# Two gated state-space convolutions on one core: fewer identity matmuls without a reader, in 26 places in place of 36

## The chip, the cores and the metric

The kernel runs on one core of a Trainium2 chip. The metric is the device time of one execution in microseconds (us); a kernel's time is the median of its runs. A core has TensorE (matmul and the load of its stationary operand), VectorE, ScalarE, GpSimd and SyncE, which here issues every DMA. The profile calls them PE and PEld, DVE, ACT, POOL and SP.

## The reference, cut to what matters

The input `x` has 2048 positions and 512 channels. Two state-space models (S4 with a pair of input and output vectors, S4D without) each make one kernel `K` of 2048 taps per channel from 128 complex modes, convolve it with the channel, and add a skip term. A gate mixes both.

```python
x = A_u
g = _sigmoid((x * gate_w).sum(-1, keepdims=True))
a = _A_ref(x, A_A_re, A_A_im, A_B_re, A_B_im, A_C_re, A_C_im, A_log_dt, A_Dskip)
b = _B_ref(x, B_log_A_real, B_A_imag, B_C_real, B_C_imag, B_log_dt, B_D_skip)
return g * a + (1 - g) * b

# inside _A_ref, and alike in _B_ref:
P = jnp.exp(logdA[:, :, None] * l[None, None, :])
K = jnp.einsum("dn,dnl,dn->dl", Cc, P, dB).real
...
Yf = Uf * Kf[None, :, :, :]
y = irfft2(Yf)[:, :, 0, :L]
y = transpose(y) + u * Dskip[None, None, :]
```

## The kernel before, in words

All arrays are float32. The 2 x 512 channels of kernels are handled in four groups of 128 channels (`q`, for the parameters) and eight half groups (`v`, 64 channels of each model). Work is staged:

- `params_t` and `params_c` make, for each `q`, angles and sizes of the modes (lines 375 to 490), from one load of raw parameters, `AB<-in_prm`.
- `anchors` makes exponentials for each `v` on ScalarE (lines 510 to 514).
- `chunk` runs eight times for each `v`. GpSimd multiplies angles and sizes out (L574, L583, L594, L602, and L560 for every fourth), ScalarE takes sines and cosines into PSUM tiles named `sd` (L614, L615, L616), VectorE multiplies both (L622, L627 into `QD`; L637, L632 into `E`), and TensorE sums over the modes with 32 small matmuls (L653, in the trace 64 records). Every second chunk ends with the skip term (L663) and a copy to SBUF (L675).
- `put` is the first half of a transform of length 2048 by matrices (L696, 32 matmuls of 64 x 64, 64 records), and `forward` the second half (L719). `stage1_u` and `stage2_u` do the same for the input `u`, whose spectrum goes to a DRAM scratch `ud` (L754, L756, L761).
- `stage2` multiplies the spectra (VectorE, L791 and L794) and begins the inverse transform (L803, L804), with the result copied (L807) to a DRAM scratch `wt` (L810).
- `gate` makes the gate's values (L865, L874, L876) and weighs the matrices of the last step with them. `final` loads `wt` back (L825), mixes both models in 32 matmul records (L836), and stores the output (L848).

The order is not written by hand. A planner, `Plan.run` (line 154), plays the operations against costs, latencies and due times and writes each engine's list of instructions. The numbers it works with were set by constants at the top of the file.

The change touches the table `FILL` (line 78). The planner counts the operations that it gives to TensorE. Where the count is a key of `FILL`, `Plan.spare` (line 140) puts matmuls ahead of that operation: the identity times a repeated identity, written to whichever PSUM tile (`ps` or `sd`) comes free first by the plan. Nothing reads the result. The value is a number of units, each 128 columns, up to four units in one matmul:

```python
for i in range(0, units, 4):
    k = min(4, units - i)
    self.keep(t[:, 0 : P * k].rearrange("p (k c) -> p k c", k=k), k)
```

All these matmuls stand on line 300 (L300 in the profile). `spare` takes no time in the plan, so its entries move no other operation; but its matmuls wait for their tile to come free like any other, and whoever writes the tile next waits for them. A float32 matmul is two weight loads and two matmuls in the trace. The PSUM tiles are six: `ps0` to `ps3` for results, `sd0` and `sd1` for sines and cosines.

Of the kernel before, what the change touches and what calls it, by code (L numbers as in the profile page):

```python
# [74 lines left out]
FW = -2.217  # L75


FILL = {1: 2, 3: 7, 5: 14, 17: 3, 49: 8, 50: 2, 51: 5, 54: 2, 55: 1, 88: 2, 160: 29, 161: 14, 162: 5, 199: 10, 201: 12, 213: 1, 275: 6, 304: 29, 22: 3, 32: 2, 33: 1, 52: 1, 53: 1, 57: 1, 58: 3, 66: 1, 68: 1, 71: 1, 181: 1, 189: 3, 196: 1, 198: 9, 200: 2, 202: 3, 244: 1, 249: 1}


def _flat(t):
# [27 lines left out]
class Plan:  # L109
# [44 lines left out]
    def run(self):  # L154
# [14 lines left out]
        while n < len(self.ops):  # L169
            nxt = 1e30  # L170
            for e in at:
# [32 lines left out]
                if e == "T":  # L204
                    if turn in FILL:
                        order.append(self.spare(FILL[turn], min((f, t, i) for t in ("ps", "sd") for f, i in free[t])))
                    turn += 1
# [842 lines left out]
```

## Time and profile before

| what | us |
|---|---|
| median of three runs | 500.5 |
| the three runs | 498.42, 500.87, 500.5 |
| the profiled execution | 499.39 |
| span of the profiled execution, first to last instruction | 497.6 |

The profile's page gives the busy time of each engine, the chain of waits that ended last, and the costliest groups of instructions. A row of the chain or of the timeline begins with the time from the span's start, then a length, both in us, then the engine, the line and what is written. Behind a row of the timeline stands in brackets how long the engine had been idle before it and what ended that. "issue" there is idle time for which the profile names no cause. `<-` reads "is made from". The transfers' page counts queue q1, which carries data, and queue q8, which carries instructions.

### The profile page before, as it was taken

The numbers are of one execution on the slowest core, as the hardware profiler recorded it, in microseconds if no ns is written. First come the engines' busy times: TensorE is split into PE (matmuls) and PEld (weight loads), VectorE is DVE, ScalarE is ACT, GpSimd is POOL, SyncE is SP. The second block draws the span as 40 slices with busy tenths as digits, with TensorE's granted clock in tenths as the row PEclk, the third lists the DMA queues.
The fourth block names the chain that finished last, engine by engine and source line by source line (L and its number), as shares of the span: only waits on it lengthen the run. The fifth ranks groups of instructions, "written<-read, shape, count | busy, mean of one in ns | idle before, by whom it ended". The sixth has DMA issues, their size and how long they took to land.

```text
span 497.6 us, 22093 instructions
## 1 busy us (share of the span) xinstructions
PE 449.3 (90%) x9718; PEld 386.4 (78%) x9718; DVE 396.6 (80%) x564; ACT 389.2 (78%) x598; POOL 394.3 (79%) x365
## 2 busy tenths in 40 slices
PE   4798897789999999999989998897999899999996
PEld 3497795678777788888568987487998799889975
DVE  5778797999939888999869988887979999884420
ACT  4679888989999887789999888786999977762111
POOL 4586986989979979999899999688979999950000
PEclk9999999999999999999999999999999999999999
DMA  8969755354554454443308676257245145863846
GB/s 278 397 195 282 218 162 157 102 167 119 157 172 141 132 178 142 127 118 119 107 4 253 184 237 237 50 199 222 67 149 177 62 130 169 268 205 108 302 141 234
DMA packets 69439, 85.46 MB, mean 172 GB/s; under 512 B 4704, under 2 KB 50144, under 8 KB 69088
## 3 DMA queue, kind: packets, MB, share of 16 engines
q1 hardware_dynamic: 69344, 84.06, 53.7%
q8 instruction: 76, 1.25, 1.1%
q14 instruction: 19, 0.16, 0.1%
HBM read 50.49 MB, written 33.59 MB: 169 GB/s over the span
## 4 chain that ended last, share of the span: by engine, by line
PE 41%; ACT 18%; DMA 16%; issue 8%; POOL 8%; DVE 8%; SPq 1%; DVEq 0%; ACTq 0%; POOLq 0%
PE ps L719 8%; PE ps L653 7%; PE ps L803 7%; PE ps L804 6%; PE ps L836 5%; PE ps L696 4%; DMA wt<-st 4%; DMA AB<-in_prm 3%; DMA c_g<-in_c_g 3%; ACT sd L614 3%; DMA X<-wt 3%; POOL E L602 2%; ACT x L615 2%; ACT sd L616 2%; DVE E L632 2%
## 5 line engine op out<-in xcount | busy, mean ns | idle before, releaser
L602 POOL TENSOR_TENSOR E<-AB 128x1024 f32<-128x1024 f32 x64 | 125.3, 1959 | 0.1
L803 PE MATMUL ps<-z,c_t 128*128 128x128 f32 x512 | 102.5, 282 | 3.7 <-DVE z L794 1.8
L804 PE MATMUL ps<-z,c_t 128*128 128x128 f32 x512 | 99.9, 277 | 0.9 <-DVE z L794 0.7
L622 DVE TENSOR_TENSOR QD<-sd,E 128x1024 f32<-128x1024 f32 x64 | 77.9, 1218 | 22.2 <-issue 7.6
L719 PE MATMUL ps<-F,c_g 128*128 128x128 f32 x640 | 83.9, 278 | 1.9 <-ACT F L708 1.2
L803 PEld LDWEIGHTS ps<-z,c_t 128*128 128x128 f32 x512 | 77.6, 191 | 8.9 <-DVE z L794 3.4
L719 PEld LDWEIGHTS ps<-F,c_g 128*128 128x128 f32 x640 | 76.2, 189 | 6.5 <-ACT F L708 1.8
L804 PEld LDWEIGHTS ps<-z,c_t 128*128 128x128 f32 x512 | 77.7, 192 | 2.6 <-DVE z L794 2.5
L632 DVE TENSOR_TENSOR E<-sd,E 128x1024 f32<-128x1024 f32 x64 | 77.8, 1215 | 0.8 <-ACT sd L616 0.8
L583 POOL TENSOR_TENSOR x<-pi,c_tm 128x512 int32<-128x512 int32 x64 | 68.0, 1064 | 11.0 <-ACT sd L616 10.1
L594 POOL TENSOR_TENSOR E<-AB 128x512 f32<-128x512 f32 x64 | 68.5, 1072 | 6.2 <-issue 2.5
L614 ACT ACTIVATE sd<-x 128x1024 f32<-128x1024 int32 x64 | 65.9, 1029 | 8.9 <-DVE QD L627 6.0
L653 PE MATMUL ps<-E 128*32 128x64 f32 x2048 | 64.7, 222 | 7.6 <-DVE E L632 3.3
L616 ACT ACTIVATE sd<-x 128x1024 f32<-128x1024 f32 x64 | 66.0, 1031 | 4.9 <-PE sd L300 2.2
L615 ACT ACTIVATE x<-x 128x1024 f32<-128x1024 int32 x64 | 67.8, 1060 | 1.3
L574 POOL TENSOR_TENSOR x<-gh 128x512 int32<-128x512 int32 x64 | 68.5, 1070 | 0.2
L807 ACT COPY st<-ps 128x512 f32<-128x512 f32 x64 | 37.6, 587 | 38.5 <-PE ps L804 24.9
L653 PE MATMUL ps<-QD 128*32 128x64 f32 x2048 | 63.5, 219 | 3.2 <-issue 3.2
L653 PEld LDWEIGHTS ps<-E 128*32 128x32 f32 x2048 | 48.2, 109 | 21.0 <-issue 10.5
L791 DVE TENSOR_TENSOR z<-ps,U 128x512 f32<-128x512 f32 x64 | 43.8, 685 | 25.0 <-PE ps L719 21.4
L653 PEld LDWEIGHTS ps<-QD 128*32 128x32 f32 x2048 | 49.9, 110 | 4.6 <-issue 4.6
L794 DVE SCALAR_TENSOR_TENSOR z<-ps,sgn,U 128x512 f32<-128x512 f32 x64 | 47.4, 742 | 0.0
(122 smaller groups left out, 786.1 us busy)
## 6 DMA issues: line engine op xcount, KB each, us to landing
U<-ud SPq DMA_DIRECT2D x32, 512.0 KB, 4.0
wt<-st SPq DMA_DIRECT2D x64, 256.0 KB, 2.9
X<-wt SPq DMA_DIRECT2D x26, 512.0 KB, 5.3
ud<-z SPq DMA_DIRECT2D x32, 256.0 KB, 3.6
U<-in_u SPq DMA_DIRECT2D x16, 256.0 KB, 4.6
ud<-z SPq DMA_DIRECT2D x32, 128.0 KB, 3.5
U<-in_uT SPq DMA_DIRECT2D x16, 256.0 KB, 3.5
out<-st SPq DMA_DIRECT2D x16, 256.0 KB, 5.4
```

The costliest lines, as they stand in the source:

```text
L574: G.tensor_tensor(xi()[:, :, 1, :].rearrange("n c (a b) -> n c a b", a=4), t[:, :, 0:4].unsqueeze(3).to_broadcast([P, NCK, 4, 8]), t[:, :, ...
L594: G.tensor_tensor(Ev()[:, :, 0, :].rearrange("n c (a b) -> n c a b", a=4), A1()[:, ca, ::-1].unsqueeze(3).to_broadcast([P, NCK, 4, 8]), BB ...
L602: G.tensor_tensor(Ev()[:, :, 1:3, :].rearrange("n c w t -> n c (w t)"), AA()[:, ca].rearrange("n c w a -> n (c w) a").unsqueeze(3).to_broa ...
L614: op("A", 0.96, e, lambda: A.activation(bv(sn), wv(xi()), AF.Sin, scale=SCL), r=[x], w=[sn], func="S")
L615: op("A", 0.96, e, lambda: A.activation(x.t, x.v(dt=I32), AF.Abs), w=[x])
L616: op("A", 0.96, e, lambda: A.activation(bv(cs), wv(qv(x)), AF.Sin, bias=HALF_PI, scale=-SCL), r=[x], w=[cs], func="S")
L622: lambda: V.tensor_tensor(ev(QD)[:, :, 0::2, :], bv(sn).rearrange("n w c t -> n c w t"), Ev()[:, :, 0::2, :], ALU.mult),
L632: lambda: V.tensor_tensor(Ev()[:, :, 0:2, :], bv(cs)[:, 0].unsqueeze(2).to_broadcast([P, NCK, 2, NJ]), Ev()[:, :, 0:2, :], ALU.mult),
L653: T.matmul(K4[32 * b : 32 * b + 32, gg, :], ev(QD if w else E)[:, c, 2, :], ev(QD if w else E)[:, c, 0:2].rearrange("n h t -> n (h t)"), s ...
L719: T.matmul(b.v("p (k m h e) -> p m k h e", k=2, m=4, h=32, e=2)[:, mm], Gw[:, m, :], Fv(F)[:, :, m, :].rearrange("p (k h) e -> p k h e", k=2),
L803: T.matmul(o, Tw[:, m, 0:128], zv(Z1), start=True, stop=False)
L804: T.matmul(o, Tw[:, m, 64:192], zv(Z2), start=False, stop=True)
```

## The change

The table has 26 entries in place of 36, and 159 units in place of 188.

```diff
-FILL = {1: 2, 3: 7, 5: 14, 17: 3, 49: 8, 50: 2, 51: 5, 54: 2, 55: 1, 88: 2, 160: 29, 161: 14, 162: 5, 199: 10, 201: 12, 213: 1, 275: 6, 304: 29, 22: 3, 32: 2, 33: 1, 52: 1, 53: 1, 57: 1, 58: 3, 66: 1, 68: 1, 71: 1, 181: 1, 189: 3, 196: 1, 198: 9, 200: 2, 202: 3, 244: 1, 249: 1}
+FILL = {1: 2, 3: 7, 5: 14, 17: 3, 49: 8, 50: 2, 51: 5, 54: 2, 160: 29, 161: 14, 162: 5, 199: 5, 201: 12, 213: 1, 275: 6, 304: 29, 22: 1, 52: 1, 58: 1, 68: 1, 189: 1, 196: 1, 198: 4, 202: 3, 244: 1, 249: 1}
```

Ten entries go (55, 88, 32, 33, 53, 57, 66, 71, 181, 200) and five shrink (199 from 10 units to 5, 198 from 9 to 4, and 22, 58 and 189 from 3 to 1). As matmuls of the program, thirteen go. In the trace of before the entries stand at these starts, in us: 22 at 44.77, 32 at 57.04, 33 at 58.95, 53 at 90.43, 55 at 95.14, 57 at 98.13, 58 at 100.20, 66 at 111.32, 71 at 118.99, 88 at 139.82, 181 at 280.73, 189 at 293.41, 198 at 308.40, 199 at 312.45 and 200 at 316.86.

No instruction of another engine moves, and TensorE's other operations keep their order. What its rows were and are is shown at three places. The number behind a tile's name is its buffer; DVE_49, Activation_49 and Pool_49 are the semaphores that VectorE, ScalarE and GpSimd raise.

TensorE at entry 32, between the input's transform (L696) and the taps (L653); `-` is before, `+` the change:

```order
 L696 MATMUL ps_101<-w_117,U_84 64x64 x2
 L696 MATMUL ps_100<-w_117,U_84 64x64 x2
-L300 MATMUL sd_105<-c_id 128x256 [waits DVE_49]
-L653 MATMUL ps_102<-E_72 32x64 [waits Pool_49]
+L653 MATMUL ps_102<-E_72 32x64 [waits DVE_49,Pool_49]
 L653 MATMUL ps_102<-E_72 32x64 x3
 L653 MATMUL ps_102<-QD_76 32x64 x4
```

The fill is gone and its wait for VectorE has moved to the first taps matmul, which waits for two engines now.

TensorE at entry 181, between the second half of a kernel's transform (L719) and the first half of the next (L696):

```order
 L719 MATMUL ps_101<-F_67,c_g 128x2x64 [waits Activation_49]
 L719 MATMUL ps_101<-F_67,c_g 128x2x64 x3
-L300 MATMUL ps_100<-c_id 128x128 [waits Activation_49]
 L696 MATMUL ps_100<-w_117,K_77 64x64 [waits Activation_49]
 L696 MATMUL ps_100<-w_117,K_77 64x64
```

Here the next operation had a wait of its own for the same engine, and keeps it.

TensorE at entry 199, between two runs of taps:

```order
 L300 MATMUL sd_105<-c_id 128x512 [waits DVE_49,Activation_49]
-L300 MATMUL sd_105<-c_id 128x512
-L300 MATMUL sd_105<-c_id 128x256
+L300 MATMUL sd_105<-c_id 128x128
 L653 MATMUL ps_102<-E_74 32x64 [waits Pool_49]
 L653 MATMUL ps_102<-E_74 32x64 x3
```

The first of the fill's matmuls and its waits stay; half of its columns are gone, and the tile sd_105, which ScalarE writes next, is free that much sooner.

## The prediction

> **What bounds the kernel now.** I read the page first, then the chain of waits in order of time, then the timeline at each place the change touches, and last the waits of TensorE. The page:
>
> ```profile
> span 497.6 us, 22093 instructions
> PE 449.3 (90%) x9718; PEld 386.4 (78%) x9718; DVE 396.6 (80%) x564; ACT 389.2 (78%) x598; POOL 394.3 (79%) x365
> PEclk9999999999999999999999999999999999999999
> q8 instruction: 76, 1.25, 1.1%
> PE 41%; ACT 18%; DMA 16%; issue 8%; POOL 8%; DVE 8%; SPq 1%; DVEq 0%; ACTq 0%; POOLq 0%
> ```
>
> TensorE is busy 90% of the span, but the chain that ended last runs through it for only 41%: ScalarE, transfers, GpSimd and VectorE carry it in turns. So an identity matmul that goes saves its length only where the chain passes through it. The chain passes through these (rows of the chain in order of time: start, length, what):
>
> ```profile
> 38.65 0.14 issue
> 44.77 0.91 PE ps L300 x2
> 57.11 0.63 PE sd L300 x2
> 59.09 0.32 PE ps L300 x2
> 60.42 1.24 issue
> 61.67 0.34 PE ps L696 x7
> 280.89 0.22 PE ps L300 x2
> 293.48 0.84 PE ps L300 x2
> 300.61 0.89 issue
> 302.29 1.98 PE ps L836 x32
> 312.45 2.39 PE sd L300 x6
> ```
>
> The two "issue" rows near 60 and 300 matter as much as the fills. At 60.42 TensorE stands still for 1.24 us in the middle of one run of L696 matmuls (57 before the gap, 7 after it), where no operand is waited for. All such stops together are in the waits of TensorE (total, times, longest):
>
> ```profile
> PE ps L653 <- issue: 5.6, 6, 2.6
> PE ps L696 <- issue: 4.5, 5, 2.1
> ```
>
> My reading is that TensorE has run out of instructions there. It executes 9718 matmuls and 9718 weight loads, 19,436 in all, and the page counts 76 instruction packets: one for every 256. In the last microseconds before both stops in the chain one such packet was moving while the data queues were full (transfers of 59.2 to 60.2 us and of 299.0 to 300.1 us):
>
> ```profile
> q8 instruction: 1, 0.02, 5.9%
> q8 instruction: 1, 0.02, 5.0%
> ```
>
> So the end of a stop is set by a packet's landing, and a TensorE that comes to the stop earlier may only stand there longer. "Runtime: NRT & Kernel Launch" of the Trainium skill, section "Instruction fetch mechanics", says the same of the blocks, 16 KiB and 256 instructions, but calls crossing them mostly hidden. By that sentence the 10.1 us of the two rows above would not be there; the trace does not agree.
>
> **The change part by part.** 29 units of 128 columns go, in 15 places. Their price: ten units take 2.39 us (chain row at 312.45) and one takes 0.49 to its end:
>
> ```profile
> 118.99 0.49 PE ps L300 x2
> ```
>
> The run-out of the last matmul is in both, so a unit takes (2.39 - 0.49) / 9 = 0.21 us. All 29 would be 6.1 us of TensorE's time, 1.2% of the span; none of it is saved unless the next operation was ready. Place by place, with what the reader should compare in the rows:
>
> ```profile
> 45.83 1.22 DVE L632 TENSOR_TENSOR E<-sd,E 128x1024 f32<-128x1024 f32 x1
> 47.40 0.32 PE L653 MATMUL ps<-E 128*32 128x64 f32 x8
> 57.04 0.70 PE L300 MATMUL sd<-c_id 128*128 128x256 f32 x2
> 57.67 0.32 PE L653 MATMUL ps<-E 128*32 128x64 f32 x8
> 58.95 0.47 PE L300 MATMUL ps<-c_id 128*128 128x128 f32 x2
> 59.34 1.08 PE L696 MATMUL ps<-w,K 64*64 64x64 f32 x57
> 280.73 0.38 PE L300 MATMUL ps<-c_id 128*128 128x128 f32 x2
> 281.05 1.16 PE L696 MATMUL ps<-w,K 64*64 64x64 f32 x64
> 314.77 0.32 PE L653 MATMUL ps<-E 128*32 128x64 f32 x8
> 314.93 1.03 ACT L616 ACTIVATE sd<-x 128x1024 f32<-128x1024 f32 x1 [2.19 <-PE sd L300]
> ```
>
> Place 44.77 (3 units to 1) frees 2 x 0.21 = 0.42 us, but the next taps matmul (L653, 47.40) needs E, which VectorE finishes at 47.05; with the 0.14 us that L653 took after L632 in the chain at 38.65 (its row is with the chain's above), 47.19 is the earliest. Gain 0.2.
>
> Places 57.04 and 58.95 go whole: 57.67 - 57.04 = 0.63 and 59.34 - 58.95 = 0.39, together 1.0 us, 2.3 us ahead of the stop at 60.42. If the packet was asked for before the fills, TensorE restarts at 61.67 all the same: gain 0. If it is asked for by something behind them, 1.0. I take 0: the packet was moving at 59.2, and a stop whose end is a landing does not shrink because one arrives early.
>
> Six places from 90 to 119 (7 units) lie where TensorE mostly waits for others:
>
> ```profile
> 95.14 0.49 PE L300 MATMUL ps<-c_id 128*128 128x128 f32 x2 [0.67 <-ACT X L708]
> 98.13 0.49 PE L300 MATMUL ps<-c_id 128*128 128x128 f32 x2 [0.71 <-ACT z L756]
> 141.23 1.12 PE L865 MATMUL ps<-U,gate_w 128*128 128x512 f32 x2 [0.82 <-DMA U<-in_uT]
> ```
>
> Most of these fills, as the two at 95 and 98, start when their PSUM bank is released; what follows gains 0.2 to 0.4 us and hands it back at the next such wait, which ScalarE's or VectorE's own queue sets. The one at 118.99 lies on the chain and could give its 0.4, until the next wait of that kind. I take 0 for the six and keep 0.4 as the other end. The two units that end at 140.4 are followed by a wait for a transfer: 0.
>
> Place 280.73: 281.05 - 280.73 = 0.3, on the chain, nothing named behind it before L836. Gain 0.3.
>
> Place 293.48 (3 to 1) frees 0.42, but L836 at 302.29 reads what two transfers issued from 293.27 bring, the slower taking 8.4 us:
>
> ```profile
> 293.27 0.85 SPq L825 DMA_DIRECT2D X<-wt  x2
> DMA to landing us min/median/max: 6.1/7.2/8.4
> ```
>
> The second (issued about 0.47 us after the first) lands at 293.74 + 8.4 = 302.1. Gain 0.
>
> Place 308.4 (9 units to 4): the next fill starts only when VectorE's L632 ends at 312.3, so 0. Place 312.45 (10 to 5): 5 x 0.21 = 1.06, and the row of ScalarE above shows who pays for the long fill: L616 waited 2.19 us for the sd tile that the fill writes. All of it on the path: gain 1.06; if GpSimd, which L653 also waits for, were late, 0. I take 1.06. Place 316.86 is not in the chain, which runs through ScalarE and VectorE there: 0.
>
> Sum of the fills: 0.2 + 0 + 0.3 + 1.06 = 1.6 us of gain; with the 1.0 of the stop at 60.42, 2.6.
>
> Then what the change moves. Up to 293 us nine matmuls have gone, 36 TensorE instructions (two loads and two matmuls each), 13 and 52 by 318. Blocks of 256 are counted from the program's start, so every later block now begins that much further on in the work. The stop at 300.61 is where this can cost. Its packet moved in 299.0 to 300.1, when the first X transfer (293.27 + 6.1 = 299.4) landed: it stood behind that one and not behind the second. A request that comes 36 instructions later (L696 runs 128 of them in about 1.1 us, so 0.3 us) may fall behind the second, issued 0.47 us after the first. Then the packet lands after 302.1 + 0.9, TensorE restarts about 1.4 us later as it did here (300.1 to 301.5), near 304.4, and L836 starts near 304.8 in place of 302.29: a loss of 2.5. Bounds 0 and 2.5; I take 2.5, since the block's shift is of the size of that margin and the fill that shrinks at 293.4 brings TensorE no closer to the load.
>
> Forecast: -1.6 + 2.5 = +0.9 us. The profiled execution took 499.39 us for its 497.6 us span; the three runs have a median of 500.5, 1.1 more, and I add to that: **501.4 us**.
>
> **The rivals.** R1, the fills' gain stands: blocks fall no worse and the stop at 60.42 ends earlier too. For it: the chain passes through all these fills. Against: that stop's end is a landing. -2.6, and the 0.4 left out above, make -3.0: 497.5. R2, the half of it: 60.42 swallows its 1.0 and no new stop appears, -1.6, 498.9.
>
> R3, slower, by one mechanism: the clock. From 308 to 315 us three fills shrink from 21 units to 9, and TensorE idles more. If the granted clock drops there, what follows runs slowly. For its price I take the first microseconds, where a two-unit fill took 1.06 us and not the 0.70 of 92.68, though the page marks no lower clock there. The third row below is a stretch without enough work (length, then TensorE's busy time, and the granted clock in the third field from the end):
>
> ```profile
> 7.18 1.06 PE L300 MATMUL ps<-c_id 128*128 128x256 f32 x2
> 92.68 0.70 PE L300 MATMUL ps<-c_id 128*128 128x256 f32 x2 [0.67 <-ACT X L708]
> 79.20:82.70 3.50, 0.89 (x50) 0.73 (x53) 1.57 (x5) 2.12 (x3) 1.65 (x3) 1.00 0.75 264
> 308.40:315.00 6.60, 5.67 (x94) 3.17 (x96) 6.57 (x8) 4.18 (x5) 6.60 (x6) 1.00 0.26 101
> ```
>
> At 1.06 / 0.70 = 1.5 times, the 5.67 us of TensorE work in such a 6.6 us stretch become 8.5, a loss of 2.8; over two of them, until fills are long again, 5.6, so -1.6 + 5.6 = +4.0 and 504.5 us. It decides from the point where idling releases the clock. Against it: 0.89 us of work in 3.5 us did not release it at 79 us, and the changed stretch keeps 5.67 - 12 x 0.21 = 3.1 us of work in about 5.5; by the trace, R3 is unlikely. The Trainium skill would put the point there: "TensorE: Matmul & The Clock Gate", section "Why this matters for your kernels", asks for no idle gap over about 3 us. The longest gap I expect in that stretch, about 2 us between the fill of four and VectorE's L632, stays under it; so does the 2.6 us of the waits quoted above, with the clock at 1.00.
>
> **How the numbers follow.** Within 0.5% of 500.5 is 498.0 to 503.0, about what a measurement of this kernel can tell from no change. The forecast (fills gain 1.6, one later block costs 2.5) has 0.44. Its own range is 499.0, where the block costs nothing or little, to 504.0, where a further block makes a stop as long as the longest seen, 2.6: I put 0.18 of it within 0.5% and 0.26 above, because 76 blocks move and the chain is tight at most of them. R1 has 0.34: 0.28 under 498.0 and 0.06 just above. R2 has 0.10, all within. R3 has 0.12, all above. So faster 0.28, within 0.18 + 0.06 + 0.10 = 0.34, slower 0.26 + 0.12 = 0.38. The range goes from a little under R1, 497.0, to a little over R3 and the forecast's upper end, 505.3.
>
> **What would show it.** In the changed profile the fill before 314.77 should be about 1.06 us shorter and ScalarE's L616 behind it should wait about 1.1 us in place of 2.19. The stop inside L696 near 60.4 should be longer, near 2.2 us, ending near 61.5. A stop ahead of L836 near 300 should have grown, or others marked "issue" in the waits of TensorE should add up to more than 10.1 us; if they add up to less, R1 holds and I am wrong on the blocks. Any stretch with a granted clock under 1.00 after the start is R3. If the work between 64 and 280 us runs more than 0.3 us ahead of before, my zeros for places 90 to 119 are wrong.

## The result, and the profile after

| | before | after |
|---|---|---|
| median, 20 runs each on one chip, us | 500.91 (497.04 to 506.38) | 504.62 (500.02 to 514.32) |
| ratio of the times | | 1.0065, interval 1.0036 to 1.0093 |
| profiled execution / its span, us | 499.39 / 497.6 | 500.02 / 498.2 |

The changed kernel is slower by 0.65%, 3.2 us. Forecast was +0.9 us, and 501.4 us in all. The median of 504.62 lies inside the whole range (497.0 to 505.3), but above the forecast's own (499.0 to 504.0). Ratios and the means further down leave disturbed runs out (over 1.5% above the fastest of their kernel); medians have every run.

The page of after, in the order in which that of before was shown:

```profile
span 498.2 us, 22043 instructions
PE 443.4 (89%) x9692; PEld 383.6 (77%) x9692; DVE 396.4 (80%) x564; ACT 388.7 (78%) x598; POOL 393.8 (79%) x365
PEclk9999899999999999999999999999999999999999
q8 instruction: 76, 1.25, 1.0%
PE 38%; ACT 20%; DMA 19%; issue 8%; DVE 7%; POOL 6%; SPq 1%; ACTq 0%; DVEq 0%; POOLq 0%
```

TensorE is busy 5.9 us less, as 29 units at 0.21 us (6.1 us) would have it, and the span is 0.6 us longer. In the chain TensorE's share has gone from 41% to 38% and that of transfers from 16% to 19%. One slice, the fifth, has a lower granted clock; before had none. This profiled execution is the shortest of the 20 runs, 4.6 us under their median, so this pair of traces can show where time is lost, and the runs must show how much.

The chain of waits of after, at the places quoted of before (start, length, what):

```profile
55.69 1.84 issue
...
292.49 1.85 PE ps L836 x29
...
296.02 8.60 DMA X<-wt
304.75 2.08 PE ps L836 x31
...
315.01 1.32 PE sd L300 x4
```

Here a transfer has come into the chain: an X load that TensorE's L836 waits for until 304.75, where before it started at 302.29. To see where it fell behind, I paired ScalarE's 598 instructions of the two traces and took the start of each in after less that in before. Its work is 0.9 us ahead at 130 us, 0.6 behind at 270, 2.6 behind at 306, 0.9 behind at 318, 0.5 ahead at 400 and 0.6 behind at 490. The loss looked into here is the 2.0 us between 270 and 306. By 318 after has 1.7 of it back, where its late fills are shorter; with the late fills as before (e3_late_back, further down) nothing comes back there (2.65 behind at 306, 2.64 at 318).

TensorE's waits of after (total, times, longest):

```profile
PE ps L653 <- issue: 3.1, 3, 2.2
...
PE ps L696 <- issue: 2.5, 3, 1.8
PE ps L836 <- DMA X<-wt: 2.2, 2, 2.0
...
PE ps L804 <- issue: 1.6, 1, 1.6
...
PE ps L836 <- issue: 0.9, 1, 0.9
```

The stops called "issue" add up to 8.1 us, less than the 10.1 before. But one of them is now in L836, and L836 waits 2.2 us for X, where before it waited 0.4. The timeline of before, around this place (the second row is SyncE's issue of the two transfers of X):

```profile
284.15 0.81 SPq L825 DMA_DIRECT2D X<-wt  x2
...
290.42 0.44 PE L836 MATMUL ps<-X 128*64 128x128 f32 x4 [0.17 <-DMA X<-wt]
...
292.05 1.12 SPq L292 DMA_DIRECT2D AB<-in_prm  x1
292.43 0.69 DVE L845 COPY st<-ps 128x512 f32<-128x512 f32 x1 [0.38 <-PE ps L836]
293.27 0.85 SPq L825 DMA_DIRECT2D X<-wt  x2
```

and of after:

```profile
284.66 0.81 SPq L825 DMA_DIRECT2D X<-wt  x2
...
291.18 0.43 PE L836 MATMUL ps<-X 128*64 128x128 f32 x3
292.49 0.32 PE L836 MATMUL ps<-X 128*64 128x128 f32 x1 [0.87 <-issue]
...
293.71 1.67 SPq L292 DMA_DIRECT2D AB<-in_prm  x1
294.37 0.69 DVE L845 COPY st<-ps 128x512 f32<-128x512 f32 x1 [1.72 <-PE ps L836]
295.49 0.91 SPq L825 DMA_DIRECT2D X<-wt  x2
...
304.75 0.43 PE L836 MATMUL ps<-X 128*64 128x128 f32 x3 [2.01 <-DMA X<-wt]
```

L836 reads X, which two transfers bring, and VectorE's L845 starts when it ends. After three of its 32 matmul records TensorE stands still for 0.87 us with all its operands there. L836 ends 1.94 us later than before (294.37 against 292.43), SyncE has its parameter load to issue first, and the next X is asked for 2.22 us later (295.49 against 293.27). That X takes 8.6 us (8.4 before), and the next L836 starts 2.46 us later. Not all of this is the stop: L836 was through at 294.3, and what held SyncE to 295.4 was the parameter load. Its issue took 1.67 us (1.12 before) and came behind a copy of ScalarE (L807) that waited 0.75 us for an earlier store. In two further kernels with this stop, e3_late_back and e11_realign_behind below, the parameter load's issue took 0.45 us, and X was asked for as soon as L836 ended.

Why a stop there? The packet of instructions that moved last before it, in 0.2 us windows of the transfers' page: of before at 285.2 to 285.4, then of after at 290.0 to 290.2 (packets, MB, share).

```profile
q8 instruction: 1, 0.02, 30.0%
```

```profile
q8 instruction: 1, 0.02, 29.3%
```

In before it began to move 1.1 us after the issue of X at 284.15, ahead of most of the two transfers' 1 MB. In after it began 5.5 us behind the issue at 284.66, when these transfers were nearly through. The change has taken 36 TensorE instructions from the program up to here, so the same block of 256 begins later in the work, and its packet came in behind a load instead of ahead of it.

That blocks lie by number and not by work can be counted in the traces. The stop at 56 to 60 us stands at TensorE's matmul 1112, counted from the start, in 12 of the 13 kept traces, and the stop in L836 stands at matmul 5822 in all three that have it (after, e3_late_back, e11_realign_behind). Neighbouring stops of that kind are 127 or 128 matmuls apart (5568, 5695 and 5822 in e3_late_back), and each matmul has a weight load beside it. What asks for a block stands in no row. If it is TensorE's entry into the block ahead, at matmul 5695, it came at 284.34 in before, between the two issues of X (284.15 and 284.58), and at 285.50 in after, behind both (284.66 and 285.09). One trace does not fit that: in e10_late_tiny_6 the entry lies between both issues too, and the packet moved 4.3 us later. So the moment of asking stays open.

### The profile page after: what moved, and what is told of

It reads as the page before. It is cut to its first block, busy times and chain, and to the rows that moved or that the text cites. A ratio compares the mean times of both kernels' runs of the same rounds, so it can differ in the third digit from the quotient of the medians.

```text
span 498.2 us, 22043 instructions
## 1 busy us (share of the span) xinstructions
PE 443.4 (89%) x9692; PEld 383.6 (77%) x9692; DVE 396.4 (80%) x564; ACT 388.7 (78%) x598; POOL 393.8 (79%) x365
## 4 chain that ended last, share of the span: by engine, by line
PE 38%; ACT 20%; DMA 19%; issue 8%; DVE 7%; POOL 6%; SPq 1%; ACTq 0%; DVEq 0%; POOLq 0%
PE ps L719 7%; PE ps L803 6%; PE ps L804 6%; PE ps L653 6%; DMA wt<-st 5%; PE ps L836 5%; PE ps L696 5%; DMA U<-in_uT 4%; ACT sd L614 4%; ACT x L615 3%; DMA X<-wt 3%; DMA c_g<-in_c_g 3%; ACT sd L616 2%; PE ps L865 2%; DMA AB<-in_prm 2%
## 5 line engine op out<-in xcount | busy, mean ns | idle before, releaser
L719 PE MATMUL ps<-F,c_g 128*128 128x128 f32 x640 | 83.9, 278 | 2.2 <-ACT X L708 0.9
L719 PEld LDWEIGHTS ps<-F,c_g 128*128 128x128 f32 x640 | 76.0, 189 | 6.5 <-issue 1.4
L632 DVE TENSOR_TENSOR E<-sd,E 128x1024 f32<-128x1024 f32 x64 | 77.6, 1213 | 0.8 <-ACT sd L616 0.8
L653 PE MATMUL ps<-E 128*32 128x64 f32 x2048 | 65.2, 223 | 7.3 <-DVE E L632 3.6
L807 ACT COPY st<-ps 128x512 f32<-128x512 f32 x64 | 37.6, 587 | 41.9 <-PE ps L804 26.6
L616 ACT ACTIVATE sd<-x 128x1024 f32<-128x1024 f32 x64 | 66.0, 1032 | 3.5 <-PE sd L300 1.1
L653 PEld LDWEIGHTS ps<-E 128*32 128x32 f32 x2048 | 48.6, 110 | 23.9 <-issue 13.2
L653 PE MATMUL ps<-QD 128*32 128x64 f32 x2048 | 63.7, 221 | 2.2 <-issue 2.2
L653 PEld LDWEIGHTS ps<-QD 128*32 128x32 f32 x2048 | 50.1, 111 | 0.0
```

What stands on the lines that cost most here:

```text
L616: op("A", 0.96, e, lambda: A.activation(bv(cs), wv(qv(x)), AF.Sin, bias=HALF_PI, scale=-SCL), r=[x], w=[cs], func="S")
L632: lambda: V.tensor_tensor(Ev()[:, :, 0:2, :], bv(cs)[:, 0].unsqueeze(2).to_broadcast([P, NCK, 2, NJ]), Ev()[:, :, 0:2, :], ALU.mult),
L653: T.matmul(K4[32 * b : 32 * b + 32, gg, :], ev(QD if w else E)[:, c, 2, :], ev(QD if w else E)[:, c, 0:2].rearrange("n h t -> n (h t)"), s ...
L719: T.matmul(b.v("p (k m h e) -> p m k h e", k=2, m=4, h=32, e=2)[:, mm], Gw[:, m, :], Fv(F)[:, :, m, :].rearrange("p (k h) e -> p k h e", k=2),
```

## The experiments

The expectations weigh two theories for the loss: the blocks (a block of 256 TensorE instructions falls badly against a load of X; theory B) and the clock (thinner fills keep TensorE's clock less well). "Small" matmuls are 32x64, unread like the others. They have as many instructions as a fill's matmul and little work. The cuts of the edits below show only the entries that differ from the kernel named in the text, after or before:

```diff
-    def spare(self, units, at):
+    def spare(self, units, at, tiny=0):
...
+            for i in range(tiny):
+                self.tiny(t[0:32, 0:64])
...
+    pl.tiny = lambda o: T.matmul(o, ident[:, 0:32], ident[:, 0:64], start=True, stop=True)
```

Every run lists its span and mean granted clock. "Lost clock" is (1 - clock) x span, and "rest" is the time less that; both are means, with their standard errors. The split is an estimate, since TensorE is not always what the end waits for; over the 91 runs of before beside the experiments, all counted, the time rises by 1.02 us per us of lost clock. "Shift" is how many TensorE instructions the program has more than before up to 290 us.

| kernel | shift | runs, median us | ratio to before, interval | lost clock | rest |
|---|---|---|---|---|---|
| before (beside the experiments) | 0 | 91 (three sets), 500.35 to 500.88 | | 2.40 ± 0.19 | 498.17 ± 0.18 |
| after | -36 | 20, 504.62 | 1.0065, 1.0036 to 1.0093 | 3.52 ± 0.58 | 500.16 ± 0.58 |
| e1_tiny | 0 | 12, 499.44 | 0.9978, 0.9944 to 1.0013 | 2.90 ± 0.52 | 496.66 ± 0.57 |
| e2_split5 | +40 | 12, 501.74 | 1.0026, 0.9995 to 1.0057 | 2.09 ± 0.52 | 499.64 ± 0.37 |
| e3_late_back | -32 | 12, 503.70 | 1.0066, 1.0033 to 1.0099 | 3.26 ± 0.47 | 500.15 ± 0.53 |
| e4_early_back | -4 | 12, 501.23 | 0.9988, 0.9953 to 1.0024 | 3.13 ± 0.77 | 496.64 ± 0.65 |
| e5_shift220 | +220 | 11, 505.85 | 1.0076, 1.0030 to 1.0122 | 1.45 ± 0.40 | 502.55 ± 0.76 |
| e6_realign | -4 | 12, 500.93 | 1.0011, 0.9979 to 1.0042 | 3.91 ± 0.25 | 497.12 ± 0.26 |
| e7_late_tiny | 0 | 12, 498.24 | 0.9978, 0.9944 to 1.0011 | 2.24 ± 0.69 | 496.53 ± 0.40 |
| e8_all_tiny | 0 | 6, 507.47 | 1.0168, 1.0131 to 1.0205 | 23.44 ± 1.34 | 484.30 ± 1.36 |
| e9_late_tiny_4 | +16 | 12, 500.93 | 1.0021, 0.9978 to 1.0065 | 3.32 ± 0.60 | 497.49 ± 0.64 |
| e10_late_tiny_6 | +24 | 12, 498.90 | 0.9963, 0.9923 to 1.0003 | 2.48 ± 0.66 | 495.63 ± 0.56 |
| e11_realign_behind | -36 | 12, 506.38 | 1.0091, 1.0052 to 1.0130 | 3.46 ± 1.09 | 501.00 ± 0.95 |

**The columns without the count.** The changed table, with each of the 13 matmuls that go kept as a small one.

```diff
+TINY = {55: 1, 88: 1, 199: 1, 32: 1, 33: 1, 53: 1, 57: 1, 66: 1, 71: 1, 181: 1, 198: 2, 200: 1}
```

> The change's columns, but each of the 13 matmuls that it removes stays as a matmul of 32 stationary and 64 moving columns, so TensorE's instructions and blocks of 256 stand where they stood before. Theory C (the clock: fewer wide matmuls let the granted clock fall in windows of about 3.4 us, each of which costs about 2 us): mean clock near 0.991 as in the changed kernel, time 504 to 505 us. Theory B (the blocks of instructions fall worse): the loss goes, 498.5 to 500 us, whatever the clock.

It took 499.44 us, ratio 0.9978: the same work left out, and no loss. So the missing columns as such cost nothing that these runs can tell from noise; what costs is that the instructions are gone.

**The count without the columns.** The kernel before, with the 14 units at entry 5 as 14 matmuls in place of four, 40 instructions more.

```diff
-            for i in range(0, units, 4):
-                k = min(4, units - i)
+            for i in range(0, units, step):
+                k = min(step, units - i)
```

> The kernel before, with its 14 units at entry 5 as 14 matmuls of one unit in place of 4 of up to four: the same columns, but 10 matmuls more, so every later block of 256 TensorE instructions begins 40 instructions earlier in the work. Theory C: same clock as before and same time within 0.3%, 500 to 502 us. Theory B: the blocks fall anew, the time moves by 2 us or more, most likely to 503 to 506 us.

501.74 us, ratio 1.0026, its interval just touching 1, rest 1.5 us above before's. The time came out as theory C had it and not at theory B's 503 to 506 us. This shift goes the other way and was not bound to hit a load; inconclusive by itself.

**One half undone.** First the five late places (entries 181 to 200) as before, then the ten early ones (22 to 88) as before:

```diff
-FILL = {199: 5, 22: 1, 189: 1, 198: 4}
+FILL = {199: 10, 22: 1, 189: 3, 198: 9, 181: 1, 200: 2}
```

> The changed kernel with entries 181, 189, 198, 199 and 200 as before (38 to 41 us of the program's middle), so that only the ten entries up to 140 us are trimmed. Theory C: the clock falls where fills were thinned out; the stretches 44 to 61 us and 90 to 101 us are still thin, so mean clock about 0.994 and 502 to 503.5 us. Theory B: the late blocks are shifted by 36 instructions, not 52: 500 to 506 us, with the clock near 1.

```diff
-FILL = {22: 1, 58: 1}
+FILL = {22: 3, 58: 3, 55: 1, 88: 2, 32: 2, 33: 1, 53: 1, 57: 1, 66: 1, 71: 1}
```

> The changed kernel with all entries up to 140 us as before, so that only 181, 189, 198, 199 and 200 are trimmed. Theory C: the thin stretch is 305 to 318 us alone: mean clock 0.994 to 0.997, and 501 to 503 us. Theory B: nothing before 280 us moves; the late blocks shift by 4 to 20 instructions; 498.5 to 503 us with the clock near 1.

With the late places back, the loss stays: 1.0066. With the early ones back it is gone: 0.9988. The early places set the shift up to 290 us, the late ones only add 4 to it. These two runs do not part the shift from the early columns, which come back with it; the next ones do. The timeline of TensorE with the late places back has the stop in L836 again, and one more ahead of it:

```profile
282.77 1.15 PE L696 MATMUL ps<-w,K 64*64 64x64 f32 x59 [1.15 <-issue]
...
293.89 0.33 PE L836 MATMUL ps<-X 128*64 128x128 f32 x2 [1.00 <-issue]
```

**The shift alone, far.** The kernel before, with 58 small matmuls and four units at entry 5 in place of 14 units.

```diff
-FILL = {5: 14}
+FILL, TINY = {5: 4}, {5: 58}
```

> The kernel before with all its columns but ten units at entry 5, which lie ahead of a wait for c_g, and 58 matmuls of 32 stationary and 64 moving columns there: TensorE has 55 matmuls or 220 instructions more, so that blocks of 256 fall 36 instructions further on in the work than before, within 6 of where the change has them from 140 to 310 us. Fills elsewhere are as before. Theory B (blocks): the time outside the clock's losses rises by 2 to 3 us over before, with the loss of about 2 us between 282 and 306 us as in the changed kernel; 502 to 504 us. Theory C (clock): 500 to 501 us.

505.85 us, 1.0076, slower, though with nothing changed behind entry 5, and slower than the 502 to 504 us expected. But its 58 small matmuls take time of their own at the start, and that part was not measured apart: it speaks for the blocks, weakly.

**The changed kernel, realigned.** The changed table, and eight small matmuls at entry 5 (near the start), 32 instructions: the blocks at 290 us lie within four instructions of where before has them.

```diff
+TINY = {5: 8}
```

> The changed kernel with one row more: 8 matmuls of 32 stationary and 64 moving columns at entry 5, ahead of the wait for c_g. All fills stay thin, but from 141 to 310 us the blocks fall within 2 instructions of where they fell before. Theory B: the time outside the clock's losses falls from 500.9 to 497 to 498 us, the median to 499.5 to 501.5. Theory C: nothing changes, 504 to 505 us.

500.93 us, 1.0011. All the shortened fills are still short, and the loss is gone. In its trace ScalarE's work is 1.7 us behind before at 270 us and still 1.7 behind at 306. One trace alone would not carry this: e1_tiny's, with the blocks in place too, falls back by 2.1 us there, behind a stop of 1.37 us and with a half-clock stretch from 302.6 to 306.0, both shown at the end. The timeline of this kernel shows L836 without a stop, held by X alone:

```profile
285.65 0.81 SPq L825 DMA_DIRECT2D X<-wt  x2
...
292.18 0.44 PE L836 MATMUL ps<-X 128*64 128x128 f32 x4 [0.43 <-DMA X<-wt]
```

Its packet began to move 0.9 us after that issue.

**The same eight, behind the place.** As a control, the eight small matmuls stand at entry 202, near 325 us.

```diff
-TINY = {5: 8}
+TINY = {202: 8}
```

> The changed kernel with the same eight small matmuls (32x64, unread) as the realigned kernel, but behind the disputed place, at entry 202 (about 325 us), so that the blocks of 256 TensorE instructions before it lie as in the changed kernel. Theory B (blocks fall badly between 282 and 306 us): the loss of about 2 us between 282 and 306 us stays, with a stop in L836 or L696 near 282 to 293 us, and the time without its lost clock stays near 500.9 us, so about 503 to 505 us in all. Rival (eight more matmuls, or any other number of instructions in the whole program, is what helped the realigned kernel): 500.9 us and no loss between 282 and 306 us.

506.38 us, 1.0091, above the 503 to 505 us expected, and the stop stands where it stood in the changed kernel:

```profile
290.92 0.43 PE L836 MATMUL ps<-X 128*64 128x128 f32 x3
...
292.27 0.32 PE L836 MATMUL ps<-X 128*64 128x128 f32 x1 [0.91 <-issue]
```

Its packet moved at 289.8, 5.6 us after X's issue at 284.18 (5.5 in the changed kernel), and ScalarE's work falls back by 2.1 us between 270 and 306. The two kernels have the same number of instructions and the same fills; where the eight stand makes the difference, and the rival, that any eight more would do, has fallen. The pair shows that the blocks ahead of 325 us cost the time; that it is at the load near 285 us rests on the traces.

**A better version.** Only the five late places shortened, their removed matmuls kept as small ones, so that nothing shifts; then with four and six small matmuls at entry 5 beside.

```diff
-FILL = {199: 10, 181: 1, 189: 3, 198: 9, 200: 2}
+FILL, TINY = {199: 5, 189: 1, 198: 4}, {181: 1, 198: 2, 199: 1, 200: 1}
```

> The kernel before with only entries 181, 189, 198, 199 and 200 trimmed as in the change, and the five matmuls that go there kept as small ones, so that no block moves. By the terms of the sum: the gain of those five entries (1.3 by the prediction) with no loss, 498.5 to 499.5 us; theory C expects a lower clock from the thin stretch at 305 to 318 us: 500.5 to 502 us.

> The kernel before with the five places from 280 to 317 us alone shortened, their removed matmuls kept as small ones (498.2 us without more), and four small matmuls (32x64, unread) added at entry 5, so that every later block begins 16 instructions earlier in the work. Theory B: the gain of the late places stays if no stop moves into the chain, 497.5 to 499 us; a further 0.3 to 0.6 us may go where stops move behind waits. Rival (the 498.2 us was the chance of one set of runs, blocks and late fills are worth nothing): 500.5 to 501 us.

> As the one before it, with six small matmuls at entry 5 in place of four (24 instructions earlier in the work). Theory B: 497.5 to 499.5 us, within 1 us of the kernel with four, since the stops at 60 and 300 us move by less than their distance to the next wait. Rival (the 498.2 us was chance): 500.5 to 501 us. If it is above 502 us, a shift of eight instructions alone has put a stop into the chain, and the blocks' effect cannot be steered this way.

498.24, 500.93 and 498.90 us; ratios 0.9978, 1.0021 and 0.9963. The middle one missed what was expected of it and came out as its rival; the last is 2 us from it, where less than 1 was expected. No interval is clear of 1. The rest is under before's by 1.6, 0.7 and 2.5 us, so the late fills' gain seems real, but a version that surely beats before was not found.

**What the fills are for.** All 67 identity matmuls made small, in their places: as many instructions, none of their work.

```diff
+FILL, TINY = {}, {1: 1, 3: 2, 5: 4, 17: 1, 49: 2, 50: 1, 51: 2, 54: 1, 55: 1, 88: 1, 160: 8, 161: 4, 162: 2, 199: 3, 201: 3, 213: 1, 275: 2, 304: 8, 22: 1, 32: 1, 33: 1, 52: 1, 53: 1, 57: 1, 58: 1, 66: 1, 68: 1, 71: 1, 181: 1, 189: 1, 196: 1, 198: 3, 200: 1, 202: 1, 244: 1, 249: 1}
```

> The kernel before with each of its 67 identity matmuls made small (32 stationary, 64 moving columns): no block moves, and TensorE has 188 units or 40 us of work less. Theory C: without the fills the clock falls in many windows, 10 or more, mean clock under 0.97, and the time is 505 us or more. Theory B alone: 492 to 497 us, with the clock as before.

1.0168: slower by 1.7%. The clock lost 23.4 us per run instead of 2.4. Two windows of its trace (length, busy times, granted clock third from the end):

```profile
244.00:248.00 4.00, 0.00 (x0) 0.00 (x0) 3.79 (x9) 3.98 (x11) 3.92 (x7) 0.99 0.31 97
248.00:261.70 13.70, 9.30 (x270) 8.57 (x270) 9.14 (x11) 13.25 (x23) 13.34 (x12) 0.50 0.05 14
```

TensorE had nothing to do in the first of them, and the next 13.7 us had half the clock. The rest fell by 13.9 us, so the fills cost this kernel some 14 us of work by this split and save 21 us of clock.

## Why the prediction was right or wrong

**The fills, forecast -1.6 us: right, -1.3.** With the blocks nearly in place (e1_tiny and e6_realign, 23 runs) the rest is 496.90 ± 0.30, against 498.17 ± 0.18; the interval of the gain is 0.6 to 2.0. The place it rested on behaved as worked out. ScalarE's timeline of after:

```profile
316.42 1.03 ACT L616 ACTIVATE sd<-x 128x1024 f32<-128x1024 f32 x1 [1.12 <-PE sd L300]
```

and TensorE's:

```profile
315.01 1.32 PE L300 MATMUL sd<-c_id 128*128 128x512 f32 x4 [2.00 <-DVE E L632]
```

The fill is 1.07 us shorter (1.32 for 2.39; forecast 1.06), L616 waits 1.12 (forecast about 1.1), and the fill still starts at L632's end, so the cut at 308.4 gave nothing. The runs agree with almost nothing for the early places: the kernels with only the late places shortened (e4_early_back, e7_late_tiny) have a rest of 496.6, no worse than those with all. A few tenths could hide in that.

**The stop near 60: the zero held by luck.** The stop at 60.42, which was to grow to 2.2 us, is gone from after's trace. Another has grown in its place, one block ahead, at the end of an L696; of before, then of after:

```profile
56.84 0.27 PE L696 MATMUL ps<-w,U 64*64 64x64 f32 x1 [0.51 <-issue]
```

```profile
57.53 0.27 PE L696 MATMUL ps<-w,U 64*64 64x64 f32 x1 [1.84 <-issue]
```

Behind it TensorE ran at half the clock for 3.4 us (the windows are shown below). At 62 us the work is 0.2 us ahead of before, against the 1.0 of the other end: the 1.0 us of fills and the 1.24 us of the old stop are gone, and the longer stop and the slow stretch took most of that back.

**Blocks, forecast +2.5 us: the mechanism right, its place wrong, its size a little small.** The prediction had a packet fall behind a load of X and L836 start near 304.8 in place of 302.29. It started at 304.75, and that this agrees so closely is luck, since the way there was another. The packet fell behind the load issued at 284.66, not the one at 293.27, and the stop hit the L836 ahead; the next load itself was then asked for late, in after's trace with the parameter load's issue on top. The stop at 300.61 is not in after's trace at all. The size by the runs: after and the control (24 runs, rest 500.44 ± 0.49) less e1_tiny and e6_realign, 3.5 us, interval 2.4 to 4.7; with after alone 3.3.

Two signs named in advance misled. The stops' total was to rise above 10.1 us or the blocks were wrong; it fell to 8.1 and they were right, because what a stop costs depends on what is queued behind it. And the work between 64 and 280 us was up to 1.1 us ahead of before, at 93 us, which was to refute the zeros for 90 to 119; but 0.7 of it was there at 80 already, and it was gone at 270. One trace's differences of this size are not bound to an edit.

**The step that failed: the sum has no term for the clock.** The clock stood in R3 alone, which was given 0.12, because the trace of before shows 1.00 throughout. That execution was not typical: in the 91 runs of before, 16 lose no or nearly no clock, and the others up to 8.5 us; a half-clock window of 3.4 us, as in the traces, costs 1.7. With the change's fills (after, e1_tiny, e6_realign, e11_realign_behind, 47 runs) the loss is 3.46 ± 0.30 against 2.40 ± 0.19: +1.1 us, interval 0.4 to 1.8. In sum, -1.3 + 3.3 + 1.1 = +3.1 us, where the ratio gives 3.2 and the forecast had +0.9. (The first two make up after's own rest, by the way in which they are taken, so that the sum comes out is no separate proof.) The median of 504.62 is next to R3's 504.5, by luck: R3 added a clock loss of 5.6 to the gain of 1.6 and had no blocks, and in after's trace the place is another too. The windows of after's trace:

```profile
55.70:57.80 2.10, 0.27 (x5) 0.20 (x9) 2.10 (x4) 0.78 (x1) 2.10 (x3) 0.99 0.50 105
57.80:61.20 3.40, 3.40 (x107) 3.21 (x110) 1.31 (x3) 2.96 (x4) 3.00 (x3) 0.50 0.59 175
...
306.00:316.50 10.50, 7.75 (x183) 5.83 (x183) 9.43 (x12) 7.17 (x11) 9.45 (x9) 1.00 0.43 130
```

The stretch it named, 308 to 315, keeps its clock. Half the clock came at 57.8, right behind the stop of 1.84 us. Which of the shortened fills cost the extra clock stays open: e3_late_back with the early ones shortened lost 3.26 ± 0.47 us, e4_early_back and e7_late_tiny with the late ones 3.13 ± 0.77 and 2.24 ± 0.69, which does not part them.

## What to carry to other kernels

An instruction that does nothing still has a place in the stream: taking it out moved every later block of 256 instructions against the transfers here. When a small edit moves the time in a way its own work cannot, put the same number of small instructions back near the start, and, as a control, behind the suspected place, before looking for another cause. And read the clock from many runs: a single profile at 1.00 does not show that the clock is safe.

## What the runs showed of the hardware that was not expected

The half-clock windows came after idle time that was shorter than expected. The Trainium skill, "TensorE: Matmul & The Clock Gate", section "Why this matters for your kernels", warns of gaps over about 3 us. The traces show shorter ones: after lost its clock behind a stop of 1.84 us. So did e1_tiny behind one of 1.37 us, which ended at 301.69; the row of its timeline and the two windows around it:

```profile
301.69 0.25 PE L658 MATMUL ps<-E 128*32 128x64 f32 x3 [1.37 <-issue]
```

```profile
300.10:302.60 2.50, 0.96 (x29) 0.61 (x17) 2.40 (x6) 1.03 (x2) 2.50 (x5) 1.00 0.94 332
302.60:306.00 3.40, 3.35 (x32) 3.31 (x32) 0.36 (x1) 2.76 (x3) 3.40 (x4) 0.50 0.08 23
```

(L658 there is L653 of the other kernels.) Yet before stood still for 2.61 us near 80 us and kept it. The same page of the Trainium skill, section "Part 1: The HAM clock gate (the "warmup" mystery)", says that activity is watched in windows of 3413 ns which run on their own. The 3.4 us from 57.8 to 61.2 and from 302.6 to 306.0 agree, and so do the starts of the half-clock stretches, which in one trace lie whole multiples of 3.413 us apart (in e8_all_tiny at 84.12, 247.96 and 319.64 us, 48 and then 21 of them). Such windows could explain why the same stop costs the clock in one run and not in another. But TensorE's busy time in a window is not all of it. These are the window ahead of after's half clock, and the one of before that holds 1.85 us of its 2.61 us stop; both have 1.57 us of matmuls, and only the first lost the clock:

```profile
54.36:57.77 3.41, 1.57 (x71) 1.24 (x71) 3.41 (x6) 2.08 (x3) 3.41 (x4) 1.00 0.66 162
```

```profile
78.44:81.86 3.42, 1.57 (x46) 0.70 (x44) 1.36 (x4) 2.54 (x5) 0.89 (x2) 1.00 0.95 328
```

What decides between the two stays open.
